# Chunked linear attention and a highway layer in one kernel: another order of all engines and loads

## The chip, the core and the metric

The kernel runs on one NeuronCore of a Trainium2 chip. Its time is the device time of one execution in microseconds. The engines are TensorE (PE), VectorE (DVE), ScalarE (ACT), GpSimd (POOL) and SyncE (SP), which here only issues DMAs. Each engine runs its own instructions in the order in which the program gives them, and waits on semaphores for the others.

## What is computed

Input are q, k and v of 4 batches, 8 heads, 768 positions and 64 channels, a decay per head, and the weights of a highway layer. All inputs and the output are float32; the kernel multiplies in bfloat16.

```python
def _attn_ref(q, k, v, lam):
    ...
    for b in range(nb):                      # blocks of 64 positions
        intra = np.einsum('bhic,bhjc->bhij', qb, kb) * Dmask[None]
        intra = np.einsum('bhij,bhjd->bhid', intra, vb)
        inter = np.einsum('bhid,bhde->bhie', qb * lam_pow[None], kv_state)
        out[:, :, sl] = intra + inter
        kb_dec = kb * rev_pow[None]
        kv_state = lam_block * kv_state + np.einsum('bhsd,bhse->bhde', kb_dec, vb)
    ...
def _moe_ref(x, w_h, w_t, b_t):              # x: attention's output, 3072 x 512
    H = np.maximum(x @ w_h, 0.0)
    T = 1.0 / (1.0 + np.exp(-(x @ w_t + b_t)))
    return T * H + (1.0 - T) * x
```

## The kernel before

The work is cut into 12 steps n: a batch has three, each of 256 positions, which are two blocks b of 128 positions. A step takes 512 KB each of q, k and v. A load takes all heads or four of the eight: `Lq.n.p` with p 0 or 1 is a half, and all q, k and v loads are halves of 256 KB. The highway weights come in four pieces of 512 KB, `W.w.g`, for the two matrices w (0: `moe_w_h`, 1: `moe_w_t`) and the two halves g of the columns.

A step goes through these operations. Names are those of the plan (below), lines those of the profile.

- `CK`, `CQ`, `CV`: k is cast, q and v are scaled by powers of the decay, into bfloat16 (L117, L119, L200). A last number 2 means all heads at once, 0 or 1 a half.
- `TK`, `TQ` (L217): PE transposes, eight products for all heads, four for a half. `EK`, `EQ` copy the result from PSUM into the tile `kq`.
- `SA`, `SB`: the scores of the step (L237) with the two updates of the state `kv` (L242) between them, which stays in one bank of PSUM. `KE` copies the state into `ss` after each. `M` (L279, on DVE) masks a bank of scores; a step has four.
- `I` (L294) multiplies the queries with the state, `A` (L305) the masked scores with v, both into one bank for each block. `D` copies this into `xT`, the transposed input of the highway layer.
- The blocks are put together in ten groups for the highway layer, of two, four or, at the end, one block. `F.g.u.w` (L331) is a block of its products, for h (w=0) or the gate t (w=1). `H` (L347) takes the relu of h less x, `G` (L354) the sigmoid of t, `X` (L357) multiplies the two. `FH`, `HH` and `XH` are smaller pieces of the last group.
- `R` (L387, L366) transposes `xT` and `X`'s result back and adds them in PSUM, `E` copies this to SBUF, `ST` (L396, L376) stores it: 512 KB for a step, smaller pieces for the last.
- `LB` computes the powers of the decay, `B` and `BC` turn the bias into a column, `WC` casts a quarter of the weights, `PT` loads the table of the sigmoid on ACT, and `Y.r` and `Z.r` are r products of 512 columns on constants whose result nobody reads (L413, L420). The text calls them idle products.

The order of all of this is one string, `PLAN`, made outside the kernel. A loop goes through its tokens and issues each, so that each engine gets its own in the order of the string; nothing reorders them later. `@` names the engine, and the digits after `=` name the buffers: in PSUM one of eight banks (`b0` to `b7`), in SBUF one of the slots of a tag, such as the five of `qf`. A token whose buffer is still read by someone waits for that reader. Loads and stores stand in SP's queue in the order of the string, too, and wait there for their slot or their data.

Of the kernel before, what the change touches and what calls it, by code (L numbers as in the profile page):

```python
# [475 lines left out]
```

## Time and profile before

| what | value |
|---|---|
| time, median of 3 runs | 106.89 us (106.44 to 107.08) |
| the profiled execution's own time | 106.81 us |
| its span, first to last instruction | 105.1 us |
| PE, DVE, ACT, POOL busy in the span | 95.2, 80.5, 69.0, 61.3 us |
| PE weight loads busy | 68.6 us |
| DMA | 27.57 MB, mean 262 GB/s |
| mean granted PE clock | 0.991 |
| idle products in the plan (`Z`) | 32, and 3 of `Y` |

A line of a timeline or of the chain begins with the start and the length in microseconds; a bracket gives the idle time of the engine before it and who ended it. "SPq" is SP issuing a DMA, "PEld" a weight load of PE. What PE is busy with is modelled at its end, so lines of successive products overlap by some tenths.

### The profile page before, as it was taken

Reading aid. Unit: us, or ns where it says so; the run is one execution under the profiler, and the core shown is the slowest. Engines: PE = TensorE matmul, PEld = TensorE weight load, DVE = VectorE, ACT = ScalarE, POOL = GpSimd, SP = SyncE. Lnnn points to the kernel's source line nnn. Section 1 sums busy time; section 2 is a strip of 40 time slices with the busy share of each in tenths; the row PEclk is TensorE's granted clock in tenths of the full one; section 3 lists DMA queues with packets and bytes.
Section 4 is the critical chain, followed back from the end, with each engine's and each line's share of the span. In section 5 each row is a group of like instructions: output and inputs, shape, how many; then the busy total and the mean of one; then the engine's idle time right before and its main releaser. Section 6 shows DMA issues by size and latency. Waiting matters only on the chain.

```text
span 105.1 us, 4749 instructions
## 1 busy us (share of the span) xinstructions
PE 95.2 (91%) x2075; PEld 68.6 (65%) x2086; DVE 80.5 (77%) x140; ACT 69.0 (66%) x118; POOL 61.3 (58%) x53
## 2 busy tenths in 40 slices
PE   6928989999599999999999999999999999999940
PEld 2405545787488888888657568665675756789930
DVE  3021692968879995989959999999799599799840
ACT  3305759435949879579798589669653867567950
POOL 6414082485469989678949999870599713300000
PEclk9999999999999999999999999999999999999996
DMA  1999999999999999999999998999996039303773
GB/s 38 303 297 288 307 329 309 288 307 329 251 306 294 297 286 291 297 291 293 297 292 298 275 308 249 313 312 340 366 379 229 16 122 349 133 6 141 256 279 128
DMA packets 43726, 27.57 MB, mean 262 GB/s; under 512 B 1462, under 2 KB 40762, under 8 KB 43706
## 3 DMA queue, kind: packets, MB, share of 16 engines
q1 hardware_dynamic: 43696, 27.27, 89.6%
q8 instruction: 16, 0.26, 1.1%
q14 instruction: 4, 0.03, 0.1%
q10 hardware_dynamic: 10, 0.00, 0.0%
HBM read 20.97 MB, written 6.29 MB: 259 GB/s over the span
## 4 chain that ended last, share of the span: by engine, by line
PE 68%; SPq 16%; DMA 7%; DVE 2%; issue 2%; ACT 1%; ACTq 0%; DVEq 0%
PE bt L331 20%; PE bh L331 17%; SPq L182 15%; DMA w_f<-in_moe_w_t_dram 7%; PE bx L387 6%; PE bo L305 5%; PE bs L237 5%; PE bktr L217 4%; PE bqtr L217 4%; PE bo L294 4%; PE kv L242 2%; SPq L186 2%; ACT ss L117 1%; PE bx L366 0%; DVE w_b L119 0%
## 5 line engine op out<-in xcount | busy, mean ns | idle before, releaser
L279 DVE TENSOR_TENSOR m<-bs,tri 128x512 bf16<-128x512 f32 x48 | 30.7, 681 | 3.9 <-PE bs L237 2.7
L331 PEld LDWEIGHTS <-w_b 128*128 128x128 bf16 x312 | 26.5, 98 | 10.7 <-DVE w_b L119 0.4
L200 POOL TENSOR_TENSOR vs<-vf,pow_v 128x1024 bf16<-128x1024 f32 (+1 forms) x12 | 21.1, 1760 | 11.6 <-DMA vf<-in_v_dram 7.4
L331 PE MATMUL bt<-xT,w_b 128*128 128x256 bf16 (+2 forms) x156 | 24.3, 292 | 0.4 <-DVE w_b L119 0.2
L331 PE MATMUL bh<-xT,w_b 128*128 128x256 bf16 (+2 forms) x147 | 23.8, 295 | 0.4
L200 POOL TENSOR_TENSOR qb<-qf,pow_q 128x1024 bf16<-128x1024 f32 (+1 forms) x12 | 21.1, 1760 | 3.3 <-DMA qf<-in_q_dram 3.3
L354 ACT ACTIVATE bt<-bt,bt_col 128x256 f32<-128x256 f32 (+2 forms) x34 | 15.5, 462 | 6.7 <-PE bt L331 4.7
L347 DVE SCALAR_TENSOR_TENSOR hm<-bh,xT 128x512 bf16<-128x512 f32 (+1 forms) x25 | 16.1, 652 | 1.7 <-PE bh L331 0.9
L117 ACT ACTIVATE xT<-bo 128x512 bf16<-128x512 f32 x17 | 12.2, 751 | 5.0 <-PE bo L305 4.8
L357 DVE TENSOR_TENSOR th<-bt,hm 128x512 bf16<-128x512 f32 (+1 forms) x19 | 12.0, 642 | 2.3 <-ACT bt L354 2.0
L237 PE MATMUL bs<-kq 64*64 64x128 bf16 x384 | 12.3, 218 | 0.0
L117 ACT ACTIVATE kq<-bktr 128x1024 bf16<-128x1024 bf16 (+1 forms) x12 | 10.3, 877 | 3.0 <-PE bktr L217 2.8
L119 POOL CAST kb<-kf 128x1024 bf16<-128x1024 f32 (+1 forms) x9 | 8.9, 990 | 3.1 <-DMA kf<-in_k_dram 3.1
L117 ACT ACTIVATE ss<-kv 128x512 bf16<-128x512 f32 x14 | 8.4, 598 | 3.4 <-PE kv L242 3.2
L357 POOL TENSOR_TENSOR th<-tb,hm 128x512 bf16<-128x512 f32 x6 | 7.0, 1161 | 5.8 <-ACT tb L354 3.1
L237 PEld LDWEIGHTS <-kq 64*64 64x64 bf16 x384 | 9.1, 107 | 1.8 <-issue 1.5
L217 PE MATMUL bktr<-id,kb 128*128 128x128 bf16 x96 | 7.7, 220 | 2.5 <-POOL kb L119 2.2
L242 PE MATMUL kv<-vs,kb 64*64 64x64 bf16 x320 | 8.8, 195 | 0.1
L117 ACT ACTIVATE kq<-bqtr 128x1024 bf16<-128x1024 bf16 (+1 forms) x7 | 6.3, 902 | 3.8 <-PE bqtr L217 3.8
L217 PEld LDWEIGHTS <-kb 128*128 128x128 bf16 x96 | 5.7, 98 | 4.4 <-POOL kb L119 2.9
L420 PE MATMUL bspin<-blank 128*128 128x512 bf16 x30 | 8.2, 410 | 0.2 <-issue 0.2
L305 PE MATMUL bo<-m,vs 64*64 64x128 bf16 x384 | 8.3, 219 | 0.1
(61 smaller groups left out, 127.8 us busy)
## 6 DMA issues: line engine op xcount, KB each, us to landing
vf<-in_v_dram SPq DMA_DIRECT2D x24, 256.0 KB, 5.5
qf<-in_q_dram SPq DMA_DIRECT2D x24, 256.0 KB, 5.1
kf<-in_k_dram SPq DMA_DIRECT2D x24, 256.0 KB, 5.5
out_dram<-o SPq DMA_DIRECT2D x11, 512.0 KB, 5.2
w_f<-in_moe_w_h_dram SPq DMA_DIRECT2D x2, 512.0 KB, 6.3
w_f<-in_moe_w_t_dram SPq DMA_DIRECT2D x2, 512.0 KB, 7.2
out_dram<-oq SPq DMA_DIRECT2D x1, 256.0 KB
out_dram<-oh SPq DMA_DIRECT2D x1, 128.0 KB, 2.2
```

The source lines that it names most:

```text
L117: A.activation(dst, src, AF.Copy)
L182: nc.sync.dma_start(out=new((x + "f", n), [128, H, J * D], F32)[:, hs], in_=SRC[x][b, hs, c * 2 * C:(c + 1) * 2 * C, :].rearrange("h (p j) ...
L200: ENG[eng].tensor_tensor(dst, in0=get(src, n)[:, heads(p)].rearrange("p h (j d) -> p h j d", j=J), in1=pw[:, n % NST, heads(p), :, None].t ...
L217: T.transpose(t[:, i, j, :], get(x + "b", n)[:, j, h:h + 2, :], id128)
L237: T.matmul(get("s", n, e, hp // 2)[half(b), hp % 2, j, :], lhsT=kq(n)[half(e), 0, hp, j, half(b)], rhs=kq(n)[half(e), 1, hp, :, half(b)], ...
L242: T.matmul(kv[half(e), hp, half(e)], lhsT=get("kb", n)[half(b), j, 2 * hp + e, :], rhs=get("vs", n)[half(b), 2 * hp + e, j, :], start=firs ...
L279: V.tensor_tensor(new(("m", n, e, u), [128, 2, J, C]), in0=get("s", n, e, u), in1=tri[:, None].to_broadcast([128, 2, J, C]), op=ALU.mult)
L305: T.matmul(get("o", n, b)[half(e), hp, :], lhsT=get("vs", n)[half(b), 2 * hp + e, j, :], rhs=get("m", n, e, u)[half(b), hp % 2, j, :], sta ...
L331: T.matmul(t[:, r, :], lhsT=w_b[w][:, kc, m * 128:(m + 1) * 128], rhs=xT(g)[:, kc, :], start=(kc == 0), stop=(kc == KC - 1))
L347: V.scalar_tensor_tensor(new(("hm", g, u), [128, len(rows(g, u)), size(g) * C], tag=f"hm{size(g)}"), in0=get("h", g, u), scalar=0.0, in1=x ...
L354: A.activation(get("tt", g, u)[:, r, :], t[:, r, :], AF.Sigmoid, bias=bt_col[:, m:m + 1])
L357: ENG[eng].tensor_tensor(new(("th", g), [128, NP, size(g) * C], tag=f"th{size(g)}")[:, span(g, u), :], in0=get("tt", g, u), in1=get("hm", ...
```

## The change

The string `PLAN` is replaced. The operations of a step, their shapes and their number are the same but for these points:

- The order of tokens on every engine and of the loads on SP's queue is another. The first loads were `Lv.0.1 Lq.0.1 Lq.0.0 Lk.1.1 Lk.1.0 Lk.0.0 Lk.0.1 Lv.0.0`; they are `Lq.1.1 Lq.0.1 Lq.0.0 Lk.0.1 Lk.0.0 Lv.0.0 Lv.0.1 Lv.1.0`.
- The engine of some copies and casts: CK on ACT, DVE, POOL was 5, 0, 9 and is 7, 2, 5; EK on ACT, DVE was 12, 2 and is 7, 7; KE was 14, 6 and is 19, 1; D was 17, 7 and is 14, 10; E was 15, 11 and is 18, 8; WC on ACT, DVE, POOL was 3, 1, 4 and is 2, 2, 4.
- The idle products: before `Z.11`, 5, 5, 3, 1, 7, now `Z.7`, 2, 3, 1, 8, 11, 3, 2, which is 37. The plan counts each at the pace of half the clock.
- `PT` stands before `KE.0.0`; before it stood ahead of `KE.2.0`.
- The last group's blocks come in another order (`FH.9.0`, `FH.9.1` last, not 2 and 3), and `store` takes an engine: the last store, `ST.11.1.4@ACT`, is issued from ACT's queue.

The diff, cut: beginning and end of both strings, and of the new one a stretch between them.

```diff
-Y.3=0 LB=6 Z.11=0 Lv.0.1=0 CV.0.1@POOL=0 Lq.0.1=0 Lq.0.0 Lk.1.1=0 CQ.0.0@DVE=0 CK.1.1@POOL=0 TK.1.1=0 TQ.0.0=1
-CQ.0.1@POOL Lk.1.0 CK.1.0@ACT Lk.0.0=1 CK.0.0@ACT=1 Lk.0.1 Z.5=2 TK.0.0=2 Lv.0.0 Lq.1.0=1 Lv.1.1=1 CV.1.1@POOL=1
-TK.1.0=3 TQ.0.1=4 EQ.0.0@DVE=0 EQ.0.1@DVE Lq.1.1 CQ.1.1@POOL=1 W.0.1 Lv.1.0 CK.0.1@ACT TK.0.1=5 EK.0.0@ACT
-EK.1.0@ACT=1 EK.0.1@ACT W.0.0 Lq.2.0=2 WC.0.1.0@POOL WC.0.0.0@POOL Lq.2.1 CQ.2.2@POOL=2 Lk.2.1=2 Lk.2.0 CK.2.2@POOL=2
-Lv.2.1=2 Lv.2.0 W.1.1 CV.2.2@POOL=2 W.1.0 WC.1.0.1@POOL WC.1.0.0@POOL Lk.3.1=3 Lq.3.0=3 Lq.3.1 CQ.3.2@POOL=0
-CV.0.0@DVE Lk.3.0 Lv.3.1=3 Z.5=1 SA.0=612 KE.0.0@ACT=0 Z.3=3 SB.0=4 CQ.1.0@DVE Lv.3.0 M.0.1.1=0 TQ.1.0=3 Lq.4.0=4
-Lq.4.1 EQ.1.0@ACT Z.1=2 TQ.1.1=5 M.0.0.0=1 M.0.1.0=2 I.0.1=2 M.0.0.1=3 WC.0.1.1@ACT A.0.1=6 CV.1.0@DVE EK.1.1@ACT
-KE.0.1@ACT=1 A.0.0 D.0.1@ACT=0 EQ.1.1@ACT Z.7=1 SA.1=134 M.1.0.0=4 D.0.0@ACT KE.1.0@ACT=2 F.0.1.0=0 WC.0.0.1@ACT
-SB.1=2 M.1.1.0=5 F.0.0.0=5 I.1.1=6 Lk.4.0=4 I.1.0=1 Lk.4.1 M.1.1.1=6 M.1.0.1=7 A.1.1 A.1.0 D.1.1@ACT=1 D.1.0@DVE
-Lv.4.1=4 B=3 Lv.4.0 KE.1.1@DVE=3 BC TQ.2.2=4 EQ.2.2@DVE=2 H.0.1=0 H.0.0=1 Lq.5.0=0 TK.2.2=2 F.1.1.0=1 EK.2.2@ACT
-CK.3.2@POOL=1 F.1.0.0=6 WC.1.1.0@DVE SA.2=342 SB.2=0 Lq.5.1 WC.1.1.1@ACT F.1.1.1=5 Lk.5.1=0 PT Lk.5.0 M.2.1.1=0
-M.2.1.0=3 KE.2.0@ACT=0 I.2.1=2 M.2.0.1=1 G.1.1 Lv.5.0=0 F.0.1.1=4 F.1.0.1=0 G.1.0 Lv.5.1 H.1.1=2 F.0.0.1=1 X.1.1@DVE=0
-Lq.6.0=1 I.2.0=5 A.2.1 M.2.0.0=2 A.2.0 G.0.1 H.1.0=2 X.1.0@DVE X.0.1@DVE=1 D.2.1@DVE=2 R.1=36 TQ.3.2=0 G.0.0 D.2.0@ACT
...
-KE.11.0@DVE=1 M.11.1.0=6 SB.11=5 M.11.0.1=0 F.6.1.1=4 I.11.0=1 ST.0 G.6.1=2 F.6.0.1=0 G.6.0 I.11.1=6 F.6.2.1=2 G.6.2
-X.6.0@DVE F.7.1.0=4 M.11.0.0=3 X.6.2@DVE F.7.1.1=5 G.7.1 H.7.1=0 ST.7 ST.6 ST.2 A.11.1 A.11.0 X.6.1@POOL R.9=03
-D.11.1@DVE=0 R.8=24 F.7.0.1=6 E.8.1@ACT=0 F.7.0.0=4 E.9.0@DVE=1 X.7.1@DVE=0 E.9.1@DVE ST.9 E.8.0@DVE ST.8 F.9.0.0=0
-D.11.0@ACT=1 F.9.0.1=5 H.7.0=2 F.8.0.1=1 F.8.0.0=3 F.8.1.1=2 G.7.0 G.9.0 X.7.0@DVE H.9.0=0 R.10=46 G.8.0 H.8.0=1
-X.9.0@DVE=0 X.8.0@DVE=1 F.8.1.0=0 H.8.1=2 G.8.1 E.10.1@ACT=4 F.9.1.1=3 R.11.1.0=5 E.10.0@ACT ST.10 FH.9.2=1 FH.9.3=0
-G.9.1 X.8.1@DVE R.11.0.2=6 E.11.1.0@ACT=0 E.11.0.2@ACT=0 ST.11.1.0 ST.11.0.2 HH.9.2=0 HH.9.3=1 XH.9.2@DVE XH.9.3@DVE
-R.11.1.5=4 R.11.1.6=1 E.11.1.5@ACT=1 E.11.1.6@DVE=2 ST.11.1.5 ST.11.1.6
+Y.3=0 LB=6 Z.7=0 Lq.1.1=0 Lq.0.1=1 CQ.0.1@DVE=0 TQ.0.1=0 CQ.1.1@POOL=1 TQ.1.1=1 EQ.1.1@ACT=0 Lq.0.0 CQ.0.0@DVE
+Lk.0.1=0 Lk.0.0 Lv.0.0=0 Z.2=2 TQ.0.0=2 CK.0.1@DVE=0 Z.3=1 TK.0.1=3 EK.0.1@DVE=1 Lv.0.1 CV.0.1@POOL=0 Lv.1.0=1
+Lk.1.0=1 Lq.1.0 Lk.1.1 Lv.1.1 Lk.2.1=2 CV.1.0@POOL=1 Lk.2.0 W.0.1 CQ.1.0@POOL WC.0.1.0@POOL W.1.1 EQ.0.1@ACT
+CK.0.0@ACT Z.1=0 TK.0.0=4 EK.0.0@ACT CV.0.0@DVE EQ.0.0@DVE Z.8=0 SA.0=561 M.0.1.1=0 M.0.1.0=1 Lq.2.0=2 Lq.2.1 W.0.0
+CQ.2.2@POOL=2 Lv.2.0=2 WC.0.0.0@POOL Lv.2.1 W.1.0 CV.2.2@POOL=2 WC.1.0.1@POOL WC.1.0.0@POOL Lq.3.0=3 Lq.3.1
+CQ.3.2@POOL=0 PT KE.0.0@ACT=0 Lk.3.0=3 CK.1.1@ACT=1 Lk.3.1 CK.3.2@POOL=2 Lv.3.0=3 Lv.3.1 CV.3.2@POOL=3 Lq.4.0=4 Lq.4.1
+Lk.4.0=4 Lk.4.1 Lv.4.0=4 Lv.4.1 CK.1.0@DVE Z.11=0 TK.1.0=0 TK.1.1=3 CV.1.1@DVE EK.1.1@DVE EK.1.0@ACT SB.0=4
+KE.0.1@ACT=1 B=2 I.0.1=1 TQ.1.0=6 Lq.5.0=1 Lq.5.1 Lk.5.1=0 Lk.5.0 EQ.1.0@ACT Z.3=0 SA.1=036 KE.1.0@ACT=2 M.0.0.1=2
+A.0.1=4 M.0.0.0=3 M.1.1.0=4 M.1.1.1=5 Z.2=5 I.1.1=5 SB.1=3 I.1.0=6 A.0.0 CK.2.2@ACT=0 M.1.0.0=6 WC.0.1.1@ACT A.1.0
+Lv.5.0=0 Lv.5.1 TK.2.2=0 M.1.0.1=7 D.0.1@ACT=0 Lq.6.0=0 Lq.6.1 EK.2.2@ACT=2 D.0.0@DVE A.1.1 BC D.1.1@ACT=1 F.0.1.0=3
+WC.1.1.0@DVE WC.0.0.1@ACT WC.1.1.1@DVE F.0.1.1=1 Lk.6.0=1 G.0.1 Lv.6.1=1 Lk.6.1 D.1.0@DVE F.1.1.0=4 TQ.2.2=2
+CQ.4.2@POOL=1 F.1.1.1=0 Lv.6.0 KE.1.1@DVE=3 F.0.0.0=6 H.0.1=0 H.1.1=1 EQ.2.2@DVE X.0.1@DVE=0 Lk.7.1=2 Lq.7.1=2 Lq.7.0
+Lk.7.0 Lv.7.1=2 Lk.9.0=3 Lv.7.0 I.2.0=5 F.1.0.0=3 G.1.1 X.1.1@DVE=1 CK.4.2@POOL=1 SA.2=421 KE.2.0@ACT=0 H.1.0=2 SB.2=0
+M.2.1.1=0 M.2.0.0=2 M.2.1.0=1 CV.4.2@POOL=0 F.1.0.1=3 G.1.0 F.0.0.1=1 G.0.0 I.2.1=4 A.2.0 Lq.8.1=3 M.2.0.1=3 A.2.1
+D.2.0@ACT=2 TQ.3.2=2 X.1.0@DVE R.1=03 H.0.0=0 CQ.5.2@POOL=2 D.2.1@DVE TK.3.2=6 EK.3.2@DVE=1 E.1.0@ACT=0 E.1.1@ACT
+X.0.0@DVE CK.5.2@POOL=0 F.2.1.0=5 F.2.1.1=4 EQ.3.2@ACT Lq.8.0 SA.3=036 KE.3.0@ACT=2 Lk.9.1 Lk.8.1=4 Lk.8.0 Lv.8.0=3
+H.2.1=1 F.2.0.1=1 G.2.0 SB.3=2 I.3.1=5 M.3.0.0=4 M.3.1.0=6 KE.3.1@ACT=1 F.2.0.0=0 G.2.1 M.3.0.1=5 M.3.1.1=7 A.3.0=3
+A.3.1 H.2.0=2 X.2.0@DVE=1 X.2.1@DVE TK.4.2=2 TQ.4.2=6 EQ.4.2@DVE=0 R.0=01 E.0.0@DVE=1 E.0.1@DVE D.3.0@ACT=1 D.3.1@ACT
+F.3.1.0=3 EK.4.2@ACT Lv.8.1 SA.4=456 KE.4.0@ACT=3 H.3.1=0 Lq.9.0=4 M.4.1.1=1 M.4.1.0=2 Lq.9.1 F.3.0.1=2 M.4.0.0=0
+F.3.0.0=0 Lv.9.1=4 H.3.0=2 Lv.9.0 Lq.10.1=1 SB.4=1 M.4.0.1=3 TK.5.2=3 CV.5.2@POOL=1 G.3.0 TQ.5.2=6 EQ.5.2@DVE=2
+KE.4.1@ACT=0 F.3.1.1=5 X.3.0@DVE=0 I.4.1=4 EK.5.2@ACT SB.5=0 SA.5=136 M.5.0.1=4 KE.5.0@ACT=2 G.3.1 CQ.6.2@POOL=0
+M.5.0.0=6 M.5.1.0=5 I.4.0=2 A.4.0 A.4.1 D.4.0@ACT=0 D.4.1@ACT CK.6.2@POOL=2 TQ.6.2=0 M.5.1.1=7 X.3.1@DVE I.5.1=1
+I.5.0=3 A.5.0 CV.6.2@POOL=2 A.5.1 D.5.1@ACT D.5.0@DVE R.2=62 TK.6.2=5 CQ.7.2@POOL=1 EK.6.2@DVE=1 E.2.1@ACT=2 E.2.0@ACT
+EQ.6.2@ACT F.4.3.1=4 G.4.3=0 F.4.3.0=3 F.4.2.0=1 H.4.2=0 SA.6=265 M.6.0.0=0 M.6.1.1=2 KE.6.0@ACT=3 H.4.3=1 M.6.1.0=1
+R.3=04 F.4.2.1=1 E.3.0@ACT=3 I.6.1=2 SB.6=0 M.6.0.1=3 CK.7.2@POOL=1 TK.7.2=5 TQ.7.2=3 EQ.7.2@DVE=0 CV.7.2@POOL=3
...
+F.4.0.0=6 H.4.0=3 TK.8.2=3 EK.8.2@DVE G.4.0 TK.9.2=2 EK.9.2@ACT=1 I.7.1=4 A.7.0 A.7.1 D.7.1@ACT X.4.0@DVE
+CV.8.2@POOL=0 SA.8=563 D.7.0@DVE M.8.1.0=0 M.8.0.0=1 Lk.11.0=1 R.4=12 E.4.0@ACT=4 KE.8.0@ACT=3 E.4.1@ACT CQ.9.2@POOL=0
+F.5.3.0=0 TQ.9.2=4 EQ.9.2@DVE M.8.1.1=2 F.5.3.1=6 F.5.2.0=1 G.5.3=2 CV.9.2@POOL=1 H.5.3=0 SA.9=524 Lv.10.0 Lv.11.0=1
...
+M.10.0.0=1 D.9.0@ACT M.10.1.0=2 F.5.0.1=6 G.5.0 Lv.11.1 I.10.0=4 ST.2 CK.11.2@ACT=0 I.10.1=1 F.5.2.1=0 X.5.0@DVE
...
+X.5.1@POOL X.6.3@POOL A.10.1 D.10.1@ACT=0 SA.11=350 KE.11.0@ACT=3 H.6.0=1 SB.11=2 M.11.0.0=3 ST.4 M.11.0.1=5
+D.10.0@DVE F.6.1.0=6 H.6.1=0 M.11.1.1=4 M.11.1.0=6 F.6.0.1=1 G.6.0 X.6.0@DVE I.11.0=3 F.6.1.1=2 G.6.1=2 X.6.1@POOL
+F.7.0.0=4 H.7.0=1 I.11.1=6 A.11.1 A.11.0 D.11.0@DVE=0 R.6=05 R.8=21 R.9=43 D.11.1@ACT=1 E.6.0@ACT=0 E.6.1@DVE ST.6
+R.7=60 E.8.1@DVE=1 E.8.0@DVE E.9.1@ACT=3 F.7.1.0=5 F.7.1.1=1 F.9.1.1=3 ST.8 E.7.1@ACT=2 E.7.0@ACT G.7.1 F.9.1.0=2
+F.7.0.1=0 H.7.1=2 X.7.1@DVE=1 ST.7 H.9.1=0 F.8.1.0=6 G.9.1 X.9.1@DVE=0 E.9.0@ACT ST.9 H.8.1=1 G.7.0 F.8.1.1=5
+F.8.0.0=1 F.8.0.1=4 G.8.1 X.7.0@DVE G.8.0 X.8.1@DVE=1 R.10=23 H.8.0=2 E.10.0@DVE=4 E.10.1@ACT ST.10 F.9.0.1=6
+R.11.1.1=0 G.9.0 FH.9.0=5 FH.9.1=4 E.11.1.1@ACT=0 ST.11.1.1 X.8.0@DVE R.11.0.2=1 HH.9.0=0 HH.9.1=1 E.11.0.2@ACT=0
+XH.9.0@DVE XH.9.1@DVE ST.11.0.2 R.11.1.3=3 R.11.1.4=2 E.11.1.3@ACT=1 E.11.1.4@DVE=2 ST.11.1.3 ST.11.1.4@ACT
@@ -370,10 +370,10 @@
         z = DM if p == 2 else DM // 2 if p < 2 else 128
         copy(eng, new(("o_sb", n, b, p), [C, z], F32, tag="oq" if p == 2 else "oh"), get("x", n, b, p))
 
-    def store(n, b, p):
+    def store(n, b, p, eng):
         i = (2 * n + b) * C
         cs = slice(0, DM) if p == 2 else slice(256 * p, 256 * p + 256) if p < 2 else slice(128 * (p - 3), 128 * (p - 2))
-        nc.sync.dma_start(out=out[i:i + C, cs], in_=get("o_sb", n, b, p))
+        (A if eng == "ACT" else nc.sync).dma_start(out=out[i:i + C, cs], in_=get("o_sb", n, b, p))
 
 
     def turns(n):
@@ -431,7 +431,7 @@
         "F": lambda a, e: block(*a), "H": lambda a, e: relu(*a), "G": lambda a, e: sigm(*a),
         "X": lambda a, e: gate(*a, e), "R": lambda a, e: turns(*a) if len(a) == 1 else turn(*a),
         "E": lambda a, e: evac_r(*a, e) if len(a) == 2 else evac_o(*a, e),
-        "ST": lambda a, e: store_r(*a) if len(a) == 1 else store(*a), "B": lambda a, e: bias(), "Z": lambda a, e: spin(*a),
+        "ST": lambda a, e: store_r(*a) if len(a) == 1 else store(*a, e), "B": lambda a, e: bias(), "Z": lambda a, e: spin(*a),
         "FH": lambda a, e: block_h(*a), "HH": lambda a, e: relu_h(*a), "XH": lambda a, e: gate_h(*a),
         "LB": lambda a, e: powers(), "Y": lambda a, e: spin_ones(*a), "PT": lambda a, e: A.preload_act_table(AF.Sigmoid),
         "BC": lambda a, e: V.tensor_copy(bt_col, get("bt")),
```

## The prediction

> **What bounds the kernel now.** I read the slices first, then the chain that ended last, then PE's timeline, then the table of stages.
>
> ```profile
> PE   6928989999599999999999999999999999999940
> PEclk9999999999999999999999999999999999999996
> DMA  1999999999999999999999998999996039303773
> ```
>
> PE is full from the twelfth slice to the last but two; the DMA engines are full for thirty slices and then half empty. So loads bound the first quarter, PE the rest. The chain shows the handover:
>
> ```profile
> 18.85 6.90 DMA w_f<-in_moe_w_t_dram
> 25.78 0.44 DVE w_b L119
> ...
> 28.37 0.40 PE bo L294 x4
> ```
>
> From 0.8 to 25.78 us the chain is SP issuing loads and the last weights landing; then it is PE. The next fence, two lines of PE's timeline and two of its weight loads', gives the holes and the pace:
>
> ```profile
> 8.23 0.40 PE L217 MATMUL bktr<-id,kb 128*128 128x128 bf16 x4 [2.18 <-POOL kb L119]
> 28.37 0.40 PE L294 MATMUL bo<-kq,ss 128*128 128x128 bf16 x4 [1.06 <-ACT ss L117]
> 3.56 0.15 PEld L420 LDWEIGHTS <-blank 128*128 128x128 bf16 x1 [0.28 <-issue]
> 4.37 1.18 PEld L420 LDWEIGHTS <-blank 128*128 128x128 bf16 x6 [0.23 <-issue]
> ```
>
> An idle product costs 0.43 us until about 4.4 us (3.13, 3.56, 3.99 are successive starts) and about 0.21 after (six loads in 1.18); the hole of 2.18 us did not bring the slow pace back. After 28.37 PE waits for nothing until 99:
>
> ```profile
> 36.00:43.00 7.00, 7.00 (x163) 6.02 (x156) 5.79 (x11) 6.17 (x12) 6.13 (x5) 1.00 1.10 291
> 64.00:71.00 7.00, 6.95 (x237) 4.97 (x236) 6.98 (x12) 5.10 (x8) 5.76 (x4) 1.00 1.00 300
> ```
>
> Columns are the stage, its length, busy PE, PEld, DVE, ACT, POOL, clock, DMA share, GB/s. PE is full in both stages; in the second DVE is full too (6.98 of 7), with no slack to lend.
>
> **A yardstick.** PE's real work is the same in both plans: 0.75 us an SA, 0.40 an SB, 0.22 an I, 0.285 an A, 0.87 an F block (0.45 in groups 8 and 9, of one row block each), 0.45 eight transposes, 0.57 an R (distances between starts in PE's timeline). Over the plan that is 85.1 us. I call "lag" the time of a PE token minus the real work before it; holes, idle products and slow pace raise it. Before: SA.0 at 12.33 with 1.4 done, lag 10.9; SA.1 17.92, 3.8, 14.1; F.0.1.1 28.60, 12.7, 15.9; F.8.1.0 ends at 99.01 with 83.3 done, lag 15.7. So the lag is settled by 28.6 and the middle adds nothing.
>
> **Part 1, loads and engines up to 28 us.** Every q, k or v load is 256 KB, a weight load two of these. Landings before, read where a user is released by its load: rank 1 at 4.02, 3 at 6.20, 4 at 7.56, 5 at 8.43, 6 at 9.34, 7 at 10.24, and the 26th unit (W.1.0) at 25.78, so 0.82 a unit. I keep the landings and change who comes at which rank; rank 2 is put between its neighbours, 5.1.
>
> New start: Lq.0.1 lands 5.1, DVE's CQ.0.1 (0.69) ends 5.8, TQ.0.1 follows; TQ.1.1 after POOL's CQ.1.1 (1.04 from 4.02); TQ.0.0 at 6.95 (6.20+0.69); CK.0.1 on DVE from 7.56, TK.0.1 about 8.1; CK.0.0 on ACT 8.43+0.63, TK.0.0 9.1 to 9.35. Lv.0.1 is now rank 7: POOL's CV.0.1 runs 10.24 to 11.28, later than EQ.0.0 on DVE (10.46), so **SA.0 starts at 11.33**, 1.0 earlier. The eight idle products before it take 1.7 of the 2.0 us there; they cost nothing at the full pace. (Counted at 0.43 they were to fill 3.4 us; at the rows' 0.21 they end early and PE idles instead.)
>
> Next: eleven idle products (2.4) run from SA.0's end, 12.1, to 14.5, where TK.1.0 could have begun at 14.0 (DVE: two masks at 0.62, then CK.1.0): 0.4 lost. Lk.1.1 (rank 11, 13.5) gives TK.1.1 at 14.75, Lv.1.1 (14.3) CV.1.1 and EK.1.1 on DVE by 15.5, SB.0, I.0.1 and TQ.1.0 by 15.95, EQ.1.0 on ACT (after KE.0.1) by 16.45, **SA.1 at 16.55** against 17.92: lag 13.2.
>
> The table load PT (1.28, which stood before KE.2.0, where the 1.06 hole is) now runs on ACT between EK.0.0 and KE.0.0, 9.9 to 11.2, while ACT waits for SA.0; uncovered it would cost up to 1.28.
>
> W.0.1 moves from units 12-13 to 15-16 (17.6), but F.0.1.0 waits longer for DVE: four masks of step 1 and D.0.0 end at 20.8. So **F.0.1.0 starts at 20.85**, lag 14.3, where before it stood at 18.67 with 14.1: nearly all the gain is gone here, to work that is done anyway. W.1.1 (19.2) and its casts on DVE end at 21.8, F.0.1.1 at once; F.1.1.0 22.75; CQ.2.2 on POOL (1.90 from 20.9) lets TQ.2.2 go at 23.65; F.1.1.1, F.0.0.0 (W.0.0 lands 22.5), I.2.0, F.1.0.0 to 27.0; CV.2.2 on POOL ends at 26.0, SA.2 and SB.2 to 28.1. W.1.0, still 26th, is cast by 27.2: no wait. **F.1.0.1 at 28.1**, 13.6 done: lag 14.55 against 15.8. The two old holes (0.24 and 1.06) are filled: **gain 1.25 us**.
>
> **Part 2, the middle.** DVE gets seven EK evacuations, ten D and two CK, ACT more KE and E; by the rows' durations DVE's sum rises by 1.6 us (79.8 to 81.4), ACT's stays, POOL's falls by 3.6. Since DVE was full in one stage, I walked each engine's order against the banks and inputs of each PE token. Waits found: F.2.1.0 for D.2.1 behind H.0.0 on DVE 0.13; SA.4 and SB.5 for evacuations 0.2; F.4.3.1 for D.5.0 0.05; F.5.3.0 for D.7.1 behind EK.9.2 on ACT 0.13. Sum **0.5 us lost**, bounds 0 (as before) and 1.5 (every close arrival, 0.3 or less to spare in some five more places, late). The last load still has four stores ahead of it on SP's queue, so it is issued near 74.4 as before; its user CV.11.2 starts after 80: hidden.
>
> **Part 3, the end.** Before:
>
> ```profile
> 99.03 0.42 DVE L347 SCALAR_TENSOR_TENSOR hm<-bh,xT 128x256 bf16<-128x256 f32 x1 [0.42 <-PE bh L331]
> 101.65 0.91 SPq L376 DMA_DIRECT2D out_dram<-oh  x2
> 101.00:102.00 1.00, 0.12 (x1) 0.00 (x0) 0.29 (x1) 0.36 (x2) 0.00 (x0) 1.00 1.02 376
> 102.00:103.00 1.00, 0.00 (x0) 0.00 (x0) 0.00 (x0) 0.00 (x0) 0.00 (x0) 1.00 1.03 369
> ```
>
> The two last stores are issued one after the other in 0.91, and the queue moves 370 GB/s: 1 MB stands behind ST.10, issued at 99.6. The store on ACT's queue saves at most one issue, 0.46. But R.10 now comes after all of group 8's blocks, and waits 0.3 for X.7.0, because G.7.0 stands behind E.9.0 on ACT; then DVE has X.8.1, H.8.0, E.10.0 (0.68) and X.8.0 before HH.9.0, and FH.9.1's bank waits for X.8.0. In work done, the last evacuation comes 1.0 later, ST.10 0.55 later, the end of the last issue 0.3 later. Bounds -0.4 (issue saved, no wait) and +1.0; I take **+0.45**, between ST.10 and the last issue, since bytes still queue.
>
> "DMA: Bandwidth & Descriptors" in the Trainium skill (Issuing engines are not separate DMA queues) says that ACT's DMAs run on the same 16 engines as SP's and save only the sequencer's time. By it, too, the gain is one issue, and none while bytes queue.
>
> **Sum.** -1.25 + 0.5 + 0.45 = -0.3 on the profiled execution: span 105.1 to 104.8, with the 1.71 around it 106.5 instead of 106.81. The median shown is 0.08 above that execution; I say **106.6 us**, own range 105.9 to 107.3.
>
> **Rivals.** (a) *Gain kept*: the four waits vanish (arrivals sooner by 0.2) and ACT's store saves its issue: 106.81-1.25-0.1 = 105.5. For it: the old plan has no wait in 70 us; against: DVE's 98% stage. 0.23. (b) *Slow pace returns*, the slower case: from 5.05 (end of Z.7) to 9.35 PE has some 2.5 us of work, in pieces. If that brings back 0.43 a product, Z.8 takes 3.4 us, SA.0 starts at 12.8, and with the pace up again all later tokens are 1.45 late: 106.6+1.45 = 108.05. It decides once Z.8 ends after 11.3, that is from six slow products on. Against: the 2.18 hole did no harm; for: the old plan was busy from 0.84 to 6 without a break, this one to 5.05. 0.15. (c) *Waits in the middle* add up: another 1.0 to 1.5, 107.6 to 108.1, where DVE, late, holds banks. 0.15. The forecast has 0.47.
>
> "TensorE: Matmul & The Clock Gate" (Part 4: PE-mode transpose) says that transposes do not count as busy. By it only six idle products, 1.3 us, count from 5.05 to 9.35, which speaks for (b); its table (Why this matters) allows gaps up to about 3 us, which speaks against. By the first the sum would be (b)'s, by the second mine; no row here shows which.
>
> **Range and chances.** A measurement of this kernel tells about 1% (1.07 us) from no change: 105.82 to 107.96. Range 105.3 to 108.1: most of (a), the forecast, (c) and half of (b), which leaves out some 0.08 on either side. Faster 0.22: (a) but for its upper edge, and a little of the forecast. Slower 0.20: 0.09 of (b), a third of (c), 0.05, and 0.06 of the forecast's far edge. Same 0.58.
>
> **What would show it.** Right: SA.0 near 11.3, SA.1 near 16.6, F.1.0.1 near 28.1 without a hole before SA.2; idle products after 5 us at 0.22; short waits on DVE's xT casts; R.10 late on X.7.0, and ST.10 nearer the end. Wrong: starts 0.43 apart in Z.8; PE waits above 1 us in the middle; a last store that lands 0.4 sooner after PE's last block.

## The result and the profile after

| | before | after |
|---|---|---|
| time, median (runs) | 106.74 us (22) | 107.43 us (22) |
| ratio to before, 95% interval | | 1.0053 [1.0027, 1.0078] |
| again on another chip | 106.83 us (35) | 106.71 us (12), ratio 0.9996 [0.9956, 1.0035] |
| profiled execution: time, span | 106.81, 105.1 us | 107.50, 105.7 us |

Executions of one program differ by two microseconds and more; the ratios leave out those more than 1.5% above the fastest of their kernel. Weighted by their intervals, the two ratios give 1.0036, some 0.4 us slower than before. The forecast was 0.3 us faster. The change makes the kernel no faster, and the gain of 1.25 us that was forecast for the start did not come.

The slices of after show PE full earlier, with a gap in the eleventh slice, and the DMA engines no longer full in the eleventh and twelfth.

```profile
PE   6998999999699999999999999999999999999950
PEclk9999999999999999999999999999999999999999
DMA  1999999999879998999999999999999500069574
```

The chain that ended last (start, length, what) now runs through v of step 2 and POOL's scaling of it:

```profile
18.80 7.54 DMA vf<-in_v_dram
26.48 1.90 POOL vs L200
28.38 0.19 POOL w_b L119
...
28.87 0.62 POOL w_b L119
...
29.54 1.92 PE bt L331 x16
```

Before, it was weights, landing at 25.78, and one cast of 0.44. Now it is a landing at 26.34, 1.90 of POOL behind it, and then POOL's two casts of the weights `W.1.0`, which end at 29.49, just before F.1.0.1. PE's timeline has the wait, and its weight loads have the pace:

```profile
28.43 0.22 PE L242 MATMUL kv<-vs,kb 64*64 64x64 bf16 x2 [1.04 <-POOL vs L200]
4.84 0.15 PEld L420 LDWEIGHTS <-blank 128*128 128x128 bf16 x1 [0.28 <-issue]
9.52 1.45 PEld L420 LDWEIGHTS <-blank 128*128 128x128 bf16 x8
```

The first line is SA.2: PE stood 1.04 us for POOL. The idle products up to 5 us were all slow (0.43), those of `Z.8` went at 0.2. The stages and the end, with the columns explained before:

```profile
36.00:43.00 7.00, 6.86 (x195) 5.35 (x183) 6.12 (x10) 5.14 (x10) 4.81 (x4) 1.00 1.01 268
64.00:71.00 7.00, 7.00 (x213) 5.06 (x213) 6.55 (x12) 5.39 (x9) 5.28 (x4) 1.00 1.06 314
101.00:102.00 1.00, 0.92 (x12) 0.52 (x9) 0.69 (x3) 0.63 (x3) 0.00 (x0) 1.00 0.83 309
102.00:103.00 1.00, 0.00 (x0) 0.00 (x0) 0.29 (x1) 0.24 (x2) 0.00 (x0) 1.00 1.01 360
```

The last lines of SP's and of ACT's timeline:

```profile
102.53 0.39 SPq L376 DMA_DIRECT2D out_dram<-oh  x1
102.36 0.38 ACTq L376 DMA_DIRECT2D out_dram<-oh  x1
```

PE now works through most of 101 to 102, where before it had finished at 101.12. The two last stores are issued side by side, but later: the last issue ends at 102.92, before at 102.56.

**Where it went, in lags.** The lag is the yardstick of the forecast; "end" is the span less the lag at F.8.1.0, "outside" the profiled execution's time less its span. The table has the profiles of the two orders, whole or with an edit that leaves the start as it is, and two more (qv2, e7) that matter below:

| profile (its run) | SA.0 | F.1.0.1 | SA.7 | F.8.1.0 | end | outside |
|---|---|---|---|---|---|---|
| forecast of after | 10.0 | 14.55 | | | before + 0.45 | 1.71 |
| before | 10.95 | 15.90 | 16.53 | 15.54 | 89.56 | 1.71 |
| before, second profile (b0) | 13.26 | 17.11 | 17.90 | 16.66 | 89.58 | 1.70 |
| before, store on ACT (b1) | 11.21 | 15.22 | 15.85 | 15.28 | 89.44 | 1.71 |
| after | 10.24 | 15.96 | 17.20 | 15.82 | 89.88 | 1.80 |
| after, second profile (a0) | 9.98 | 15.46 | 16.64 | 15.61 | 89.85 | 1.81 |
| after, last store on SP (e4) | 9.77 | 15.12 | 16.27 | 14.89 | 89.96 | 1.84 |
| after, E.9.0 on DVE (e3) | 9.76 | 15.18 | 16.33 | 14.96 | 89.71 | 1.99 |
| after, two copies on ACT (e5) | 9.87 | 14.43 | 15.83 | 15.72 | 89.89 | 2.08 |
| after, less v in step 2 (qv2) | 10.04 | 14.55 | 15.79 | 14.41 | 89.88 | 1.80 |
| after, halves and E.9.0 (e7) | 10.57 | 14.63 | 15.46 | 14.32 | 89.70 | 2.07 |

SA.0 comes 0.4 to 1.45 earlier in the profiles of after's order (b0 left out), around the 1.0 of the forecast. At F.1.0.1 the five profiles with after's start lie between 14.43 and 15.96, those of before between 15.22 and 17.11: what is left of the gain differs from execution to execution by more than it is worth. The column "outside" is of one execution for each kernel; experiment 9 has all of them.

### The profile page after: what moved, and what is told of

Read it like the earlier page. It is cut to its first block, busy times and chain, and to the rows that moved or that the text cites. A ratio compares the mean times of both kernels' runs of the same rounds, so it can differ in the third digit from the quotient of the medians.

```text
span 105.7 us, 4778 instructions
## 1 busy us (share of the span) xinstructions
PE 98.6 (93%) x2091; PEld 70.0 (66%) x2091; DVE 82.5 (78%) x143; ACT 69.2 (65%) x119; POOL 57.8 (55%) x49
## 4 chain that ended last, share of the span: by engine, by line
PE 53%; SPq 16%; DVE 10%; DMA 7%; issue 4%; ACT 3%; POOL 3%; DVEq 0%; POOLq 0%
PE bt L331 14%; SPq L182 14%; PE bh L331 12%; DMA vf<-in_v_dram 7%; PE bx L387 5%; PE bo L305 5%; PE bs L237 4%; PE bktr L217 3%; PE bqtr L217 3%; DVE m L279 3%; PE bo L294 3%; SPq L186 3%; DVE th L357 2%; ACT bt L354 2%; PE kv L242 2%
## 5 line engine op out<-in xcount | busy, mean ns | idle before, releaser
L331 PE MATMUL bh<-xT,w_b 128*128 128x256 bf16 (+2 forms) x152 | 24.4, 298 | 0.0
L354 ACT ACTIVATE bt<-bt,bt_col 128x256 f32<-128x256 f32 (+2 forms) x34 | 15.4, 460 | 6.2 <-PE bt L331 5.0
L117 ACT ACTIVATE ss<-kv 128x512 bf16<-128x512 f32 x19 | 11.3, 594 | 10.0 <-PE kv L242 10.0
L117 ACT ACTIVATE xT<-bo 128x512 bf16<-128x512 f32 x14 | 10.2, 749 | 2.5 <-PE bo L305 2.5
L420 PE MATMUL bspin<-blank 128*128 128x512 bf16 x37 | 10.8, 427 | 0.0
L117 ACT ACTIVATE o<-bx 128x512 f32<-128x512 f32 x15 | 8.4, 595 | 1.5 <-PE bx L387 1.3
L242 PEld LDWEIGHTS <-kb 64*64 64x64 bf16 x320 | 7.0, 109 | 3.4 <-issue 2.9
L217 PE MATMUL bqtr<-id,qb 128*128 128x128 bf16 x96 | 7.8, 225 | 0.3
L117 ACT ACTIVATE kq<-bqtr 128x1024 bf16<-128x1024 bf16 (+1 forms) x7 | 5.8, 842 | 3.5 <-PE bqtr L217 3.4
```

The source lines that it names most:

```text
L117: A.activation(dst, src, AF.Copy)
L217: T.transpose(t[:, i, j, :], get(x + "b", n)[:, j, h:h + 2, :], id128)
L242: T.matmul(kv[half(e), hp, half(e)], lhsT=get("kb", n)[half(b), j, 2 * hp + e, :], rhs=get("vs", n)[half(b), 2 * hp + e, j, :], start=firs ...
L331: T.matmul(t[:, r, :], lhsT=w_b[w][:, kc, m * 128:(m + 1) * 128], rhs=xT(g)[:, kc, :], start=(kc == 0), stop=(kc == KC - 1))
L354: A.activation(get("tt", g, u)[:, r, :], t[:, r, :], AF.Sigmoid, bias=bt_col[:, m:m + 1])
```

## The experiments

Times are medians; "before" is that of the same chip. What a run leaves out is in its expectation.

| run | time | before | ratio, 95% interval |
|---|---|---|---|
| e1_v2_halves | 106.35 | 106.32 | 1.0027 [0.9999, 1.0055] |
| e2_v2_halves_wact | 106.53 | 106.32 | 1.0018 [0.9983, 1.0052] |
| e3_e9_dve | 106.80 | 106.32 | 1.0052 [1.0011, 1.0093] |
| e4_last_sp | 106.70 | 106.32 | 1.0033 [1.0000, 1.0067] |
| b1_act_store | 106.53 | 106.85 | 0.9972 [0.9939, 1.0006] |
| b2_v2_late | 108.08 | 106.85 | 1.0079 [1.0037, 1.0121] |
| e5_mid_act | 107.86 | 106.85 | 1.0112 [1.0064, 1.0160] |
| e6_all | 106.77 | 106.85 | 0.9993 [0.9961, 1.0025] |
| q2_before | 105.62 | 106.83 | 0.9909 [0.9873, 0.9945] |
| q2_after | 106.15 | 106.83 | 0.9934 [0.9900, 0.9967] |
| a0_again | 106.71 | 106.83 | 0.9996 [0.9956, 1.0035] |
| b0_again | 106.75 | 106.83 | 1.0009 [0.9965, 1.0053] |
| qv2_after | 106.49 | 106.69 | 1.0026 [0.9991, 1.0060] |
| qv2_before | 105.97 | 106.69 | 0.9986 [0.9951, 1.0021] |
| e7_halves_e9 | 106.76 | 106.69 | 1.0028 [0.9989, 1.0067] |
| b3_more_idle | 106.41 | 106.69 | 0.9986 [0.9944, 1.0028] |
| o1_dve8 | 107.73 | 107.06 | 0.9999 [0.9943, 1.0054] |
| o2_act4 | 107.80 | 107.06 | 1.0028 [0.9972, 1.0085] |

**1. Is v of step 2 late because POOL takes it whole?** e1 gives POOL one half and DVE the other; e2 also moves a cast of the weights off POOL.

```diff
-... CV.2.2@POOL=2 WC.1.0.1@POOL WC.1.0.0@POOL ... X.0.1@DVE=0 ... CK.4.2@POOL=1 SA.2=421
+... CV.2.1@POOL=2 WC.1.0.1@POOL WC.1.0.0@POOL ... X.0.1@DVE=0 CV.2.0@DVE ... CK.4.2@POOL=1 SA.2=421   (e1)
+... CV.2.1@POOL=2 WC.1.0.1@POOL ... X.0.1@DVE=0 CV.2.0@DVE ... CK.4.2@POOL=1 WC.1.0.0@ACT SA.2=421    (e2)
```

> The changed kernel, with step 2's v scaled in two halves: the first on DVE, between X.0.1 and X.1.1, the second on POOL (1.04 instead of 1.90 us). Theory A (the gain of the start was lost because v of step 2 lands at 26.3 and its scaling on POOL ends at 28.4): SA.2 starts about 27.4 instead of 28.43, F.1.0.1 about 29.0 instead of 29.54, since W.1.0 lands at 27.8 and POOL casts both its halves; the span falls by some 0.5 to about 105.2 and the ratio to the kernel before goes from 1.005 to about 1.000. Rival B (DVE is full between 36 and 48 us, so what the start gains is given back there): SA.2 is as early, but PE is no earlier from 50 us on, and the ratio stays at 1.005.

> As the kernel with halves of v, and one of the two casts of W.1.0 goes to ACT, ahead of KE.2.0. Theory A: F.1.0.1 about 28.5 instead of 29.54, span about 104.8, ratio about 0.996. Rival B: F.1.0.1 as early, PE at 50 us where it was, ratio 1.005.

F.1.0.1 started at a lag of 15.08 in e1 and 14.42 in e2, against 15.96 in after. The span of e1 was 104.6, and its twelve times lie between 105.90 and 106.95. But against before nothing is won. In e1 F.1.0.1 no longer waits for v but for `W.1.0`, which landed at 27.38: its two casts on POOL ended at 28.60, and F.1.0.1 started at 28.66. In e2, with one of these casts on ACT, it started at 28.00. In e2's profile the lag rose again from 15.43 at SA.8 to 16.32 at SA.10, behind loads of steps 9 and 10.

**2. The end.** e3 takes E.9.0 from ACT, so that G.7.0 need not wait behind it; e4 gives the last store back to SP, and b1 gives the last store of before to ACT.

```diff
-E.9.1@ACT=3 F.7.1.0=5 ... X.9.1@DVE=0 E.9.0@ACT ST.9
+E.9.1@ACT=3 E.9.0@DVE F.7.1.0=5 ... X.9.1@DVE=0 ST.9       (e3)
-ST.11.1.3 ST.11.1.4@ACT
+ST.11.1.3 ST.11.1.4                                        (e4)
-ST.11.1.5 ST.11.1.6
+ST.11.1.5 ST.11.1.6@ACT                                    (b1, in before)
```

> The changed kernel, with E.9.0 on DVE, right after E.8.0, instead of on ACT ahead of G.7.0. If the end's loss is G.7.0, X.7.0 and R.10 standing behind E.9.0 (forecast, 0.3 on R.10): X.7.0 is 0.5 earlier, R.10 runs without its wait, the last evacuation and the span are 0.3 to 0.5 earlier, ratio about 1.001. If the end is bound by the bytes behind ST.10, or by DVE's chain after it: less than 0.2, ratio about 1.004 to 1.005.

> The changed kernel, with the last store back on SP's queue. If ACT's queue saves an issue: the last issue ends 0.4 later (about 103.3 instead of 102.9), span 0.3 to 0.4 longer, ratio about 1.008 to 1.009. If the end is set by the bytes in the queue: span the same, ratio 1.005.

> The order of the kernel before, and only its last store issued from ACT's queue. Theory (a store's queue is worth nothing, because SP is idle at the end and the packets take the same time): 106.7 +- 0.3 us, as before, and the span less the lag of the last F products within 0.1 us of before. Rival (two issues side by side save up to 0.4 us): 106.3 us. It is also a second profile of the order before: if executions differ by about 1 us in the landing of the loads, F.1.0.1 will not start at 29.48 again but up to 1 us earlier, at a lag between 14.9 and 15.9.

The end was 89.88 in after, 89.70 and 89.71 in e7 and e3, 89.96 in e4 and 89.44 in b1 (before: 89.56). So E.9.0 on ACT costs 0.17 of the 0.32 by which the end is longer, and the store on ACT's queue saves 0.1. What makes up the rest, some 0.25, no run shows. In e4 SP issues both last stores, in one line:

```profile
101.61 0.89 SPq L376 DMA_DIRECT2D out_dram<-oh  x2
```

That is 0.5 more than the 0.39 in after, and the end is 0.1 longer. For b1 the time alone could have been read as the rival's 0.3; its end says 0.1, and the interval of its ratio does not exclude that.

**3. Does a later v of step 2 cost before, too?**

```diff
-Lk.2.0 ... Lv.2.1=2 Lv.2.0 W.1.1 CV.2.2@POOL=2 W.1.0
+Lk.2.0 ... W.1.1 Lv.2.1=2 Lv.2.0 CV.2.2@POOL=2 W.1.0
```

> The order of the kernel before, with the block W.1.1 of the weights loaded ahead of the two halves of v of step 2, which is how the kernel after has them. Theory (the landing of v of step 2, behind it POOL's copy, is what sets the lag at SA.2 and F.1.0.1): the halves land about 0.9 us later, and the kernel is 0.5 to 0.9 us slower than before, 107.3 us. Rival (the lag comes from the order of TensorE and VectorE, the landing has slack): within 0.2 us of before.

The kernel is 0.8% slower: the landing has no slack in the old order either. The halves landed at 24.51 and 25.72 instead of 22.30 and 23.04 (23.65 and 24.53 in b0). In the profiled execution (109.28 us) the clock fell to half as well, from 27.98 to 31.40, behind the longer wait at SA.2. The ratio does not come from that: the seven executions behind it have mean clocks of 0.991 to 0.998, the profiled one 0.979.

**4. The middle.**

```diff
-R.0=01 E.0.0@DVE=1 E.0.1@DVE D.3.0@ACT=1 D.3.1@ACT F.3.1.0=3 EK.4.2@ACT Lv.8.1
+R.0=01 D.3.0@ACT=1 D.3.1@ACT F.3.1.0=3 EK.4.2@ACT E.0.0@ACT=1 E.0.1@ACT Lv.8.1
```

> The kernel after with the two result copies E.0.0 and E.0.1 on ACT behind EK.4.2 instead of on DVE between 37.6 and 47 us. Theory of the middle (VectorE is the chain there: two copies of about 0.5 us in front of X.3.0 and the masks of step 4): the lag between SA.3 and SA.5 rises by 0.3 to 0.6 us less than in after, 107.0 us against 107.4. Rival (the lag of the middle is given back anyway, because the loads of steps 9 and 10 or the end bind): same as after within 0.2 us.

The theory fell: from SA.3 to SA.4 the lag rose by 0.80 (after 0.74), and the kernel is the slowest variant of after. DVE's chain there is not made of these two copies. One piece of the 0.6 by which after is worse at SA.7 can be named. In the four profiles with v of step 2 in halves (e1, e2, e6, e7) the lag rises by only 0.3 to 0.4 from SA.3 to SA.4 (0.7 to 0.8 in the others), and by 0.75 to 0.9 from F.1.0.1 to SA.7. There DVE's X.2.0 follows H.2.0 at once; in the other seven profiles of after's order DVE stands idle for 0.5 before it (DVE's timeline in after, then in e1):

```profile
40.09 1.29 DVE L357 TENSOR_TENSOR th<-bt,hm 128x512 bf16<-128x512 f32 x2 [0.53 <-DVE hm L347]
```

```profile
38.79 1.29 DVE L357 TENSOR_TENSOR th<-bt,hm 128x512 bf16<-128x512 f32 x2
```

Why the halves take this wait away is not shown, and the rest of the 0.6 stays open. The profile of e5 then lost 0.87 between SA.7 and SA.8, in a wait that after does not have:

```profile
65.22 0.22 PE L242 MATMUL kv<-vs,kb 64*64 64x64 bf16 x2 [0.81 <-POOL vs L200]
```

The load behind it, Lv.8.1, was issued as early as elsewhere (56.78) but landed 2.16 behind the load in front of it, where most other profiles have 0.7 to 0.9 (e6 1.43).

**5. All together, and the two that helped.** e6 is e2, e3 and e5 in one, e7 is e1 and e3.

> The kernel after with four edits together: v of step 2 copied in halves by POOL and DVE, WC.1.0.0 on ACT, E.9.0 on DVE, E.0.0 and E.0.1 on ACT. If the three lost terms are what keeps after behind (start 1.3, middle 0.5, end 0.45 us) and add up: 105.7 us, about 1 us under before. If the loads of steps 9 and 10 bind once TensorE is early (rival, first seen in one profile of the halves with WC.1.0.0 on ACT): 106.4 us, no better than before, with the lag rising by 0.5 us or more between SA.8 and SA.10 behind a load that lands just before its copy.

> The kernel after with the two single edits that shortened a term each: v of step 2 copied in halves by POOL and DVE, and E.9.0 on DVE. Theory (the terms add up): 0.6 us under after, 106.2 us, ratio to before 0.996 to 0.999. Rival (loads of later steps take the gain back): ratio 1.002 as with the halves alone.

The spans of the profiled executions are the shortest of all with full loads, 103.9 and 104.0, 1.7 below after's, but these executions are among the fastest of their kernels (105.89 and 106.09 us); the medians are level with before. The lag did not rise between SA.8 and SA.10 in either, so in these two executions the loads of steps 9 and 10 took nothing. Part of the gain is lost outside the span: over all executions that is 1.98 us in e6 and 2.09 in e7, against 1.73 in before (experiment 9). So the single repairs do not add up to a version that beats before.

**6. Less to load.** In q2 all loads of q, k and v from step 2 on are a quarter as long, in qv2 only those of v of step 2.

```diff
+        t = new((x + "f", n), [128, H, J * D], F32)
+        if n >= 2:                     # qv2: if x == "v" and n == 2
+            hs = slice(hs.start, hs.start + 1)
-        nc.sync.dma_start(out=new((x + "f", n), [128, H, J * D], F32)[:, hs],
+        nc.sync.dma_start(out=t[:, hs],
```

> The order before, but every load of steps 2 to 11 brings one head of its four and the casts read that head four times (the output is therefore another one; instructions, shapes and order of all engines stay). Supply theory (how late the loads land, with stalls of about 1 us that fall at other places in each execution, decides the lag in the first 30 us and again at steps 8 to 10): faster than before by 1 us or more, 105.5 us, and its runs lie closer together. Rival (the order of the engines sets the time, the loads have slack): within 0.3 us of before.

> The order after with the same one head of four in every load of steps 2 to 11 (another output). Supply theory: the lag at F.1.0.1 falls to 14.0 or less, against 14.4 to 16.0 in the profiles with full loads; without the loads what is left between the orders is the start's own gain (0.8) against the middle (0.5) and the end (0.45), so it comes within 0.3 us of the order before with the same loads, either side. Rival (the order itself is 0.7 us worse): 0.5 us or more behind the order before with the same loads.

> The kernel after, in which only the two loads of v of step 2 bring one head of four and CV.2.2 reads that head four times (another output); all other loads whole, so POOL's work does not move onto DVE's casts of the weights. Theory (start): the halves land by 24.0 us instead of 24.8 to 26.3, CV.2.2 ends by 26.0, the lag at F.1.0.1 is 14.4 or less against 14.4 to 16.0, and the kernel is 0.6 us or more under after, 106.3 us: ratio to before 0.995 to 0.998. Rival (v of step 2 has slack, the rest of the order sets it): as after, ratio 1.003 to 1.005.

> The kernel before with the same two loads at one head of four (another output). There the lag of F.0.1.1 hangs on W.1.1 behind these loads, which then lands about 1.3 us earlier. Theory: 0.3 to 0.6 us under before, less than after gains, because POOL's order puts CQ.2.2, CK.2.2 and CV.2.2 one behind the other: ratio 0.995 to 0.997. Rival: no change, ratio 1.000.

q2 makes both orders faster, by 0.9 and 0.7%: loads still set part of the time. But the lag at F.1.0.1 in q2_after was 15.4, not the 14.0 or less that I expected, and so q2 does not test the start. POOL, served early, ran beside two casts of the weights on DVE (timelines of DVE and of POOL in q2_after, then DVE's in e5):

```profile
20.45 2.71 DVE L119 CAST w_b<-w_f 128x512 bf16<-128x512 f32 x2
20.23 1.90 POOL L210 TENSOR_TENSOR qb<-qf,pow_q 128x1024 bf16<-128x1024 f32 x1 [1.03 <-DMA qf<-in_q_dram]
```

```profile
20.21 0.75 DVE L119 CAST w_b<-w_f 128x512 bf16<-128x512 f32 x2
```

2.71 us instead of 0.75 for the pair: F.1.1.0 came 1.4 later for it.

qv2_after is the nearer test. Lv.2.1 landed at 23.70, near the 24.1 of the forecast, the wait at SA.2 was gone, and the chain into F.1.0.1 has POOL's q and PE alone:

```profile
21.92 1.91 POOL qb L203
23.84 0.05 issue
23.88 0.62 PE bqtr L227 x8
24.50 0.87 PE bt L341 x8
25.37 0.87 PE bh L341 x8
```

The lag at F.1.0.1 was 14.55, the forecast's figure to the digit. So the walk through the engines was right for such landings, and the landings were wrong. The run does not set v apart from `W.1.0`, which came earlier, too (25.22, in after 27.76).

The time does not follow, though. The kernel's median was 0.2 us below before's on its chip, but the ratio, 1.0026, is the one that I gave to the rival (1.003 to 1.005) and not to the theory (0.995 to 0.998). Before's median with the same loads is lower, too (105.97; by the ratio no difference is resolved). In both pairs the old order stays ahead: by the medians 0.5 us, by the ratios 0.3 us in q2 and 0.4 in qv2. The end (0.32) and the time outside the span (0.06), which do not hang on loads, make about that.

**7. Two kernels unchanged, for the spread.**

> The kernel after unchanged, for a further profile and for the ratio on one chip. Both theories: ratio 1.005. If stalls of transfers of about 1 us wander from execution to execution, the lag at F.1.0.1 is between 14.4 and 15.2 and not 15.96 as in the first profile of after, unless a stall falls on v of step 2 again.

> The kernel before unchanged, a further profile of it on the same chip. Supply theory: ratio 1.000, the lag at F.1.0.1 between 14.5 and 15.9, not the same as in the first profile (15.90) where W.1.1 landed 2.7 us behind the load in front of it. Rival (the landings are the same in every execution): 15.9 again.

In a0 the lag at F.1.0.1 was 15.46, a little outside what I expected, with Lv.2.1 at 25.84; in the nine profiles with full loads and this order of loads it landed between 24.81 and 26.34. b0's lag was already 13.26 at SA.0, and only 0.3 of that came from its loads (the hole ended at 8.53 instead of 8.23). Four stages of it, with the clock in the third column from the end:

```profile
8.00:9.00 1.00, 0.47 (x7) 0.48 (x8) 0.00 (x0) 0.28 (x1) 1.00 (x2) 0.90 1.13 287
9.00:10.00 1.00, 1.00 (x7) 0.45 (x5) 0.42 (x1) 0.77 (x2) 0.47 (x1) 0.50 1.10 286
11.00:12.00 1.00, 0.94 (x7) 0.47 (x5) 0.00 (x0) 0.09 (x1) 0.00 (x0) 0.50 1.00 273
12.00:13.00 1.00, 1.00 (x16) 0.88 (x14) 0.29 (x1) 0.84 (x2) 0.00 (x1) 0.89 1.08 329
```

The clock fell to half at 8.81 and came back at 12.22. That is what rival (b) of the forecast said of after, but in the kernel before.

**8. Is it the hole in TensorE's start?** `Z.11=0` became `Z.15=0` in before.

> The kernel before with 15 idle products in its first group instead of 11, which fill part of the hole of TensorE between 6.0 and 8.2 us. Theory (in some executions of before the granted clock falls to 0.5 between 8.9 and 12.2 us behind that hole, as the second further profile showed, and these are its runs above 107.4 us): fewer runs above 107.4 us, about 1 of 12 instead of 1 of 3, median 0.2 us lower. Rival (the fall comes by chance): the same share of such runs, median within 0.1 us or later by up to 0.4 us, because the products end behind the landing of the first k.

Five of fourteen runs lay above 107.4, against eight of 35 of before; the theory's one in twelve did not show. The mean clocks of the executions decide it. One stretch of 3.41 us at half the clock takes 0.016 off the mean. Of before's eight long executions one is that low (108.68 us, 0.984), the others have 0.990 to 1.000; b3's five have 0.991 to 1.000. So the fall of the clock is not what makes most of the long executions long.

**9. What lies outside the span.** `J` copies four columns of the empty tile, on DVE or ACT.

```diff
-Y.3=0 LB=6 Z.11=0 Lv.0.1=0
+Y.3=0 LB=6 Z.11=0 J.8@DVE Lv.0.1=0      (o1; o2: J.4@ACT)
```

> The kernel before with eight copies of four columns of the empty tile on DVE between 3.4 and 6.2 us, where DVE is idle; nothing reads them, the output is the reference's. What lies outside the span (time of the profiled execution less its span) was 1.70 to 1.71 us in every profile of before's order and 1.80 to 2.08 in the variants of after, growing by 0.09 with each further DVE instruction in after, e1, e3 and e7. Theory (it grows with DVE's instructions): 2.4 us here, and the time 0.7 us longer at the same span. Rival (it hangs on something else in the layout of the program): 1.7 to 1.8 us, time as before within 0.3 us.

> The kernel before with four such copies on ACT between 3.8 and 8.4 us, where ACT is idle; the output is the reference's. Theory (ACT's instructions count, as e5 and e6 with the most of them suggest, 2.08 and 1.96 us): 1.9 to 2.1 us outside the span, time 0.2 to 0.4 us longer. Rival: 1.7 us, time as before.

In the profiled executions o1 had 2.36 us outside the span, o2 1.71 as before. The instruction counts stand in the first part of o1's page (before: DVE x140):

```profile
PE 98.0 (93%) x2086; PEld 69.1 (65%) x2086; DVE 82.8 (78%) x148; ACT 68.9 (65%) x118; POOL 61.4 (58%) x53
```

That seems to bear out the theory, but every execution has its span on record (to 0.1 us), and the other nine of o1 had 1.77 to 1.85, 1.81 in the mean. Over 153 executions of before it is 1.73 in the mean, 1.65 to 1.87 in the single ones. So the eight instructions cost some 0.08 us together, and the 2.36 is of one execution; after has one such, too, 2.42 among 34. The rival's 1.7 to 1.8 held. The ratios agree: 1.000 and 1.003, with intervals of half a per cent.

## Why the forecast was wrong, point by point

**The failing step is the landing of v of step 2, and of the last weights behind it**, in part 1, "the 26th unit (W.1.0) at 25.78, so 0.82 a unit". The weights that end before's chain at 25.78 are W.1.1, the 24th unit; W.1.0 landed at 27.29. SP, DVE and POOL show it in before:

```profile
18.85 1.67 SPq L186 DMA_DIRECT2D w_f<-in_moe_w_t_dram  x2
25.78 0.43 DVE L119 CAST w_b<-w_f 128x512 bf16<-128x512 f32 x1 [0.51 <-DMA w_f<-in_moe_w_t_dram]
27.34 1.17 POOL L119 CAST w_b<-w_f 128x512 bf16<-128x512 f32 x2 [2.27 <-DMA w_f<-in_moe_w_t_dram]
```

SP issues W.1.1 and then W.1.0; by the plan DVE casts a quarter of W.1.1, and POOL both quarters of W.1.0. From rank 7 at 10.24 to rank 24 at 25.75 that is 0.91 a unit. At 0.82 Lv.2.1, now the 24th unit, should land at 24.1; at 0.91 it is 25.7, and it landed between 24.81 and 26.34. POOL's 1.90 behind it made "CV.2.2 on POOL ends at 26.0" into 28.38, and SA.2 1.4 late. "W.1.0, still 26th, is cast by 27.2: no wait" fell with it: W.1.0 landed at 27.76, its casts behind v on POOL ended at 29.49, and F.1.0.1 started at 29.54. The row in the chain gave a line and a time, but not which of the two loads of that line; the order of the issues would have told.

**The start**, −1.25: measured as +0.06 in the first pair of profiles (15.96 against 15.90); the median of after's five is 15.18, 0.7 under that pair's before and level with the best of before (15.22). SA.0 (11.39 for 11.33) was right, SA.1 (16.97 for 16.55) 0.4 late, F.0.1.0 (21.03 for 20.85) nearly right again: DVE's masks and D.0.0 end at 20.74, where the forecast had 20.8. qv2 shows that at such landings the lag is the forecast's. The base of the gain was one execution, too: in before's profile W.1.1 landed 2.71 behind the load ahead of it, and the lag was 15.90; in b1, with 1.62, it was 15.22. Against that the forecast's 14.55 is a gain of 0.7.

**The middle**, +0.5: after loses 1.15 to 1.24 between F.1.0.1 and SA.7, before 0.63 to 0.79, so 0.5 is right there. Up to F.8.1.0 most of it comes back: −0.2 to +0.15 in after, −0.45 to +0.06 in before. The four waits I named are not among PE's listed waits, and moving two copies off DVE (e5) did not help. The list has nothing below 0.2, so waits as short as those would hardly stand in it. The sum was near; its reasons are not shown, and the one wait that the runs do show, DVE's 0.5 before X.2.0, was not among the four.

**The end**, +0.45: measured +0.32 (89.88 against 89.56). Right in sign and near in size, and in part for the reasons given: E.9.0 ahead of G.7.0 accounts for 0.17 of it (e3), and the store on ACT's queue for a gain of 0.1 (e4, b1), where 0.46 was the most that I allowed. That the bytes queue fits the 360 GB/s that moved between 102 and 103.

**Outside the span**: I took 1.71 for both. Over all executions it is 1.73 in before and 1.79 in after (the one of 2.42 left out): +0.06.

**The sum.** Taking the end and the outside from each median leaves the lag at F.8.1.0 that start and middle made: 106.74 − 1.73 − 89.5 = 15.5 for before, 107.43 − 1.79 − 89.9 = 15.7 for after; on the second chip 15.6 and 106.71 − 1.79 − 89.9 = 15.0. So start and middle gave something between +0.2 and −0.6 where I had −0.75, and end and outside took 0.4 back. In the first pair of profiles (106.81 and 107.50) the forecast missed by 0.99: the start by +1.31, the middle, taken up to F.8.1.0, by −0.28, the end by −0.13, and the time outside by +0.09. So the start is the term that failed.

**The rivals.** (a) "Gain kept" did not come. (b) did not come in after: in all its profiles the clock, once full (from 5.3 to 7.4 us on), stayed so for as long as PE had work. (c) was right in sign at SA.7, but small. The forecast's largest risk, the loads' landing itself, was no rival: all cases kept the same landings.

## What to carry to other kernels

When a chain ends in a load, find out by the order of issues which load it is before making a rate of it, and then ask how far the landing moves between executions: here a load that must land at 24.1 for the plan came between 24.8 and 26.3. A gain at a point where the stream of loads is the bound is a gain only if the load that PE needs there moves up in the stream. One profile of each kernel is not a comparison when executions differ by more than the change; use quantities that do not depend on the spread, such as the end measured from a late token, and look for a quantity in every execution on record before taking it from the one with a profile.
